# RWKV recurrence with two feed-forward stages on one core: decay of the state moved to ScalarE, a smaller gate, no constant products, scans two chunks ahead

## The chip, the cores and the metric

The kernel runs on one core of one Trainium2 chip. The metric is the device time of one execution in microseconds. Engines are named as in the profile: PE is TensorE (PEld its weight loads), DVE VectorE, ACT ScalarE, POOL GpSimd, SP the queue that issues most transfers.

## The reference

Three stages follow one another, over 4 x 768 tokens of width 384 (8 heads of 48).

```python
# 1. recurrence, for every batch b and head h, with a 48 x 48 state
for t in range(S):
    cur = np.einsum('bhd,bhe->bhde', u[None] * kt, vt)
    y[:, :, t] = np.einsum('bhd,bhde->bhe', rt, state + cur)
    state = wt[:, :, :, None] * state + np.einsum('bhd,bhe->bhde', kt, vt)
# 2. one of 8 experts per token, for tokens whose skip score is above 0
logits = xc @ w_gate; e_idx = argmax(logits); gate_w = softmax(logits)[e_idx]
out = xc + gate_w * (relu(xc @ w1[e]) @ w2[e])
# 3. dense: h = x @ w_in; g = h * clip(h + 3, 0, 6) / 6; return g @ w_out
```

## The kernel before

The change lies in the first stage. It cuts the 768 steps into 6 chunks of 128 and takes them in the order chunk, batch: 24 pieces, numbered i, four to a round (one chunk of all four batches). Inside a piece the recurrence is products: with running products p of the decay w, the score matrix of a piece is (k scaled) by (r scaled), masked, times v, plus r times the state left by the piece four earlier.

One pass of the main loop works on several pieces at once, and the order of the code is the order on each engine (manual schedule). Per pass the engines do this:

- DVE: `state` adds the new outer products (in PSUM tile `sl`) to the old state (L569), and multiplies by the decay of the whole chunk (L573); `scan` forms the forward running product (L431), four pieces ahead of the state; `scan_end` bounds its last value from below (L436), `scan_inv` takes the inverse (L439), `scan_back` runs four scans backward (L446, four instructions); `masked` (L494, twice) evacuates the scores; `x_out` (L546) adds the diagonal part. Each fourth pass the gate's first half `gate_a`, each fourth its second, `gate_o` and `gate_b`, come in between.
- PE: `scores` (L490), four products of constants into the bank of the result (L524), `apply` in two halves (L529 with the state, L534 with v), `xpose` (L583) between the halves, `k_xpose` (L504, L507), `state_mm` (L558, L560), `logits` (L597), and each fourth pass `gate_rank`.
- ACT: `diag_v` (eight scaled copies, L478), copies of the state into the two diagonal blocks `sbd` (L574, L575), the decay `pc` (L467), evacuations (L585, L511, L514), and `w_hi` (L270), the upper half of an expert's weight.
- POOL: `scale` (L456, the products of r and k with p), `ru` (L470), a `scatter` of 128 finished tokens to their expert's rows (L663), and `w_lo` (L276), the lower half of a weight, in 12 passes from the tenth on.
- SP: loads of a piece's r, k and w (`ch`, 3 buffers), of v, of raw weights, stores of the result, and in passes 2 to 5 zero rows for the scatter's target.

After the last piece the gate of the last chunk is done in two halves (batches 0 and 1, then 2 and 3), the last tokens are scattered, and the second stage loads them (`xw`), transposes them (L815 to L817) and multiplies. There the weights' lower halves are formed on DVE.

Of the kernel before, what the change touches and what calls it, by code (L numbers as in the profile page):

```python
# [19 lines left out]
E, F = 8, 1024  # L20
# [16 lines left out]

P_LO = 1e-16
# [4 lines left out]
DG = 2  # L43
W0 = 7
# [165 lines left out]
def rwkv_moe_kernel(ctx: ExitStack, tc: tile.TileContext, ch, vt, u, w9, wx, wm, out):  # L210
# [19 lines left out]
    cum = const.tile([128, E1], BF16, name="cum")  # L230
# [114 lines left out]
    with tc.manual_schedule():  # L345
# [8 lines left out]
        nc.vector.memset(cum, 0.0)  # L354


        with ExitStack() as p1:
            wpool["raw"] = p1.enter_context(tc.tile_pool(name="rawp", bufs=3))
# [42 lines left out]
            one, zero, pgp = cb[0:PP, 0:1], cb[0:PP, 1:2], cb[0:PP, 8:12]  # L401
            dkp = cb[:, 16:48].rearrange("p (b e) -> p b e", b=B)
            cmp_, s4p, cumf, stp = cb[:, 48:52], cb[:, 52:56], cb[:, 64:73], cb[0:PP, 128:320]
            stp = stp.rearrange("p (a d) -> p a d", a=PR)
            sl = ps_s.tile([128, 512], F32, tag="sl", name="sl")
            st = [fx.tile([PP, PR, D], F32, name=f"st{b}") for b in range(B)]
            cdt = [fx.tile([128, B, E1], F32, name=f"cd{j}") for j in range(2)]
            sbd = [fx.tile([PP, PR, 2 * D], F32, name=f"sbd{b}") for b in range(B)]
# [3 lines left out]
            nc.vector.memset(cumf, 0.0)  # L412
# [6 lines left out]
            for t in cdt:  # L419
                nc.vector.memset(t, 0.5)  # L420
            nc.gpsimd.iota(ids, pattern=[[C, NCH], [S, B]], base=0, channel_multiplier=1)
            nc.gpsimd.iota(zrow[:, 385:386].bitcast(I32), pattern=[[0, 1]], base=BIGI, channel_multiplier=1)

            pw, pcw, rtw, ktw, ruw, dgw, dvw, atw, ktT, xt4, lgp, xTs, scw, xw, rkw_ = ({} for _ in range(15))
# [36 lines left out]
            def scale_rest(i):  # L461
                rc = chb.pop(i)
                rkw_.pop(i)
                pe = pw.pop(i)[1]
                if i // B < NCH - 1:
                    pc = wk.tile([PP, PR], F32, tag="pc", name="pc", bufs=4)
                    nc.scalar.activation(out=pc, in_=pe, func=ACTF.Copy)  # L467
                    pcw[i] = pc
                ru = wk.tile([PP, PR, C], F32, tag="ru", name="ru", bufs=3)
# [92 lines left out]

            def state(i):
                c, b = divmod(i, B)
                if c < NCH - 1:
                    sp = sl[0:PP, 0:PR * D].rearrange("p (a d) -> p a d", a=PR)
                    pcb = pcw.pop(i).to_broadcast([PP, PR, D])
# [6 lines left out]
                    nc.scalar.activation(out=sbd[b][0:48, :, 0:D], in_=st[b][0:48], func=ACTF.Copy)  # L574
                    nc.scalar.activation(out=sbd[b][64:112, :, D:2 * D], in_=st[b][64:112], func=ACTF.Copy)  # L575
                elif ok(i + 4):
                    scan(i + 4)
# [10 lines left out]
            def logits(i):  # L588
                c, b = divmod(i, B)
                xT = xTs.pop(i)  # L590
                b0 = 2 if i >= NST - 2 else 0
# [9 lines left out]


            def gate_a(c, b0, nb):
# [10 lines left out]
                ex = sm.tile([128, B, E], F32, tag="ex", name="ex")[:, 0:nb, :]  # L614
                nc.scalar.activation(out=ex, in_=dl, func=ACTF.Exp)
                cd = cdt[(c + b0 // 2) % 2][:, 0:nb, :]
# [4 lines left out]
                od = sm.tile([128, B, E1], BF16, tag="od", name="od")[:, 0:nb, :]  # L621
# [4 lines left out]
            def gate_rank(c, b0, nb):  # L626
# [4 lines left out]
                nc.tensor.matmul(rnk, ones, cum[:, None, :].to_broadcast([128, nb, E1]), start=True, stop=False)  # L631
# [5 lines left out]


            def gate_o(c, b0, nb):
                ex, od = gw.pop((c, b0))  # L640
                o1 = sm.tile([128, B, E1], F32, tag="o1", name="o1")[:, 0:nb, :]
                nc.vector.tensor_tensor(out=o1, in0=rkw.pop((c, b0)), in1=od, op=ALU.mult)
                gw[c, b0] = ex, od, o1

            def gate_b(c, b0, nb):
                xt = xt4[c][:, b0:b0 + nb, :]
                ex, od, o1 = gw.pop((c, b0))
                s4 = s4p[:, 0:nb]
                nc.vector.tensor_reduce(out=s4, in_=ex, axis=AX.X, op=ALU.add)
                nc.vector.tensor_scalar(out=s4, in0=s4, scalar1=1e-9, scalar2=None, op0=ALU.add)  # L650
                nc.vector.reciprocal(out=xt[:, :, DM], in_=s4)
                si = sm.tile([128, B], I32, tag="si", name="si")[:, 0:nb]
                with nc.allow_low_precision(reason="one term of the sum is not zero, a whole number"):
                    nc.vector.tensor_reduce(out=si, in_=o1, axis=AX.X, op=ALU.add)
                siw[c, b0] = si
                sd = sm.tile([128, E1], F32, tag="sd", name="sd")
                nc.vector.tensor_reduce(out=sd, in_=od.rearrange("p b e -> p e b"), axis=AX.X, op=ALU.add)
                nc.vector.tensor_tensor(out=cumf, in0=cumf, in1=sd, op=ALU.add)
                nc.vector.tensor_copy(out=cum, in_=cumf)

            def scatter(c, b):
                b0 = 2 if c == NCH - 1 and b >= 2 else 0
# [4 lines left out]

            wq = [(0, q) for q in ORD] + [(1, q) for q in range(4)]
            rq = list(wq)
# [4 lines left out]
            for i in range(-3, NST + 1):  # L674
                if i >= W0 + 2 and wq:
                    w_hi(*wq[0])
# [6 lines left out]
                if ok(i + 3):  # L683
                    scan_end(i + 3)
                    scan_inv(i + 3)
                    if i + 3 > 0:
                        scan_back(i + 3)
                if i == -3:
# [3 lines left out]
                    scale_rest(0)  # L692
                if i == 1 - 3:
                    scale(1)
                    scale_rest(1)
# [5 lines left out]
                if i == -1:  # L701
                    scores(1)
                    for g in range(2):
                        masked(1, g)
                if ok(i + 2) and i >= 0:
                    scale(i + 2)
                    scale_rest(i + 2)
                if 7 <= i < NST - 1:
                    scatter(*divmod(i - 7, B))
                if i == NST - 1:  # L710
                    for b in range(B):
                        scatter(NCH - 2, b)
                if i < 2 - 3:
                    load_ch(i + 3 + 3)
                if ok(i + 5) and i >= 0:
                    load_ch(i + 5)
                if i >= 6 and (i - 6) % 4 == 0 and i < NST:
                    gate_o((i - 6) // 4, 0, B)
                if i > 0 and ok(i + 1):
# [6 lines left out]
                if i >= W0 + 2 and wq:  # L726
                    w_lo(*wq.pop(0), nc.gpsimd)
                if i >= W0 and rq:
                    w_raw(*rq.pop(0))
                if i >= 5 and (i - 5) % 4 == 0 and i < NST:  # L730
                    gate_a((i - 5) // 4, 0, B)
                if i >= 6 and (i - 6) % 4 == 0 and i < NST:
                    gate_b((i - 6) // 4, 0, B)
                if i > 0 and ok(i + 1):
# [6 lines left out]
                if ok(i):  # L741
# [3 lines left out]
                if i == NST - 1:  # L745
                    logits(i - 2)
                    gate_a(NCH - 1, 0, 2)
                    logits(i - 1)
                elif ok(i - 1) and i < NST - 2:
                    logits(i - 1)  # L750
                if i >= 5 and (i - 5) % 4 == 0 and i < NST:
# [5 lines left out]
                for k in range(1, i + 6) if i == -3 else (i + 5,):  # L757
                    if ok(k):
                        load_v(k)
            gate_rank(NCH - 1, 0, 2)  # L760
            gate_o(NCH - 1, 0, 2)
            gate_b(NCH - 1, 0, 2)
            logits(NST - 1)
            for b in range(2):
                scatter(NCH - 1, b)
            warm1(4, "sc0")
            for f in (gate_a, gate_rank, gate_o, gate_b):
                f(NCH - 1, 2, 2)
            for b in range(2, B):
                scatter(NCH - 1, b)  # L770
            warm1(4, "sc0")

# [208 lines left out]
        def flag_sum():  # L981
            p = ps.tile([128, 512], F32, tag="tp1", name="fs")[0:1, 0:E1 + 2]
            nc.tensor.matmul(p[:, 0:E1], ones[:, 0:1], cum, start=True, stop=True)
# [93 lines left out]
```

## Time and profile before

| | |
|---|---|
| median of 3 runs | 760.44 us (758.36 to 762.3) |
| profiled execution, its own time | 762.69 us |
| span of the profiled execution | 761.0 us |
| granted TensorE clock over the span | 0.988 |
| PE, DVE, ACT, POOL busy | 734.3, 497.3, 346.9, 219.0 us |

The profiled execution is 2.25 us above the median; 1.69 us of its time lie outside the span. The recurrence takes the first 159 us or so, the experts and the dense stage the rest. Shares of busy time mix these stages, so the rows further down are taken from the stretches that the change touches.

### The profile page before, as it was taken

To read this page: it belongs to the slowest core of one execution; us is meant where nothing else is said; L and a number is where in the kernel's file an instruction comes from. 1 tells how busy PE (TensorE), PEld (TensorE's weight loads), DVE (VectorE), ACT (ScalarE), POOL (GpSimd) and SP (SyncE) were. 2 spreads that over 40 slices of the span, in tenths; PEclk is the share of its full clock that TensorE was granted. 3 is DMA by queue.
4 is the path that set the end of the run, shared out by engine and by line. 5 is a ranking of instruction groups with operands and counts; after the bars stand their busy time and mean duration, and the time that the engine had idled before them with its cause. 6 is when DMAs were issued, how large, how long until landed. Compare 5 with 4: busy or idle time off the path is not lost.

```text
span 761.0 us, 14589 instructions
## 1 busy us (share of the span) xinstructions
PE 734.3 (96%) x5653; PEld 604.8 (79%) x5653; DVE 497.3 (65%) x974; ACT 346.9 (46%) x796; POOL 219.0 (29%) x192
## 2 busy tenths in 40 slices
PE   7999999989999997989999999999999999999995
PEld 3788888859999997957777888888888888788884
DVE  8989999837999999927885454455445434333331
ACT  2666777626566666326554333333233333333331
POOL 3758999942344444303441000000000000000000
PEclk9999999999999999989999999999999999999998
DMA  8699888328787873042230220221022010001001
GB/s 233 206 300 264 246 243 251 112 86 287 249 276 238 288 250 143 13 159 62 85 103 13 77 68 13 79 66 37 2 90 67 25 54 1 1 0 43 0 1 46
DMA packets 40590, 90.84 MB, mean 119 GB/s; under 512 B 5442, under 2 KB 19552, under 8 KB 40512
## 3 DMA queue, kind: packets, MB, share of 16 engines
q1 hardware_dynamic: 37952, 85.14, 36.6%
q0 software_dynamic: 2560, 4.69, 1.7%
q8 instruction: 46, 0.75, 0.4%
q14 instruction: 32, 0.26, 0.1%
HBM read 72.51 MB, written 20.53 MB: 122 GB/s over the span
## 4 chain that ended last, share of the span: by engine, by line
PE 69%; DVE 21%; DMA 3%; ACT 2%; issue 2%; SPq 1%; POOL 0%; DVEq 0%; ACTq 0%
PE f L787 8%; PE f L788 8%; PE f L790 8%; PE acc L950 8%; PE acc L952 8%; PE acc L949 8%; DVE wlo L276 5%; PE sc L490 4%; PE x L534 3%; PE x L529 3%; PE x L524 2%; DVE wlo L327 2%; DVE hl L828 2%; DVE a L304 2%; DVE a L307 2%
## 5 line engine op out<-in xcount | busy, mean ns | idle before, releaser
L935 DVE SCALAR_TENSOR_TENSOR f<-t,f 128x512 f32<-128x512 f32 x96 | 66.6, 694 | 130.5 <-ACT t L934 130.5
L934 ACT ACTIVATE t<-f,three 128x512 f32<-128x512 f32 x96 | 66.0, 688 | 160.1 <-PE f L790 160.1
L950 PE MATMUL acc<-gh,wlo 128*128 128x512 f32 x288 | 115.0, 399 | 2.0 <-DVE wlo L327 1.8
L787 PE MATMUL f<-bh,whi 128*128 128x512 f32 x288 | 115.6, 401 | 0.6 <-ACT bh L922 0.6
L949 PE MATMUL acc<-gh,whi 128*128 128x512 f32 x288 | 115.7, 402 | 0.0
L788 PE MATMUL f<-bh,wlo 128*128 128x512 f32 x288 | 115.1, 400 | 0.0
L937 DVE TENSOR_TENSOR gl<-f,gh 128x512 fp32r<-128x512 f32 x96 | 66.4, 691 | 63.8 <-ACT gh L936 63.8
L936 ACT ACTIVATE gh<-f 128x512 fp32r<-128x512 f32 x96 | 57.4, 598 | 100.3 <-DVE f L935 100.3
L952 PE MATMUL acc<-gl,whi 128*128 128x512 f32 x288 | 84.0, 396 | 0.0
L790 PE MATMUL f<-bl,whi 128*128 128x512 f32 x288 | 83.6, 399 | 0.0
L950 PEld LDWEIGHTS acc<-gh,wlo 128*128 128x128 f32 x288 | 54.3, 188 | 17.5 <-DVE wlo L327 5.5
L314 POOL TENSOR_TENSOR lf<-lf,ab 128x384 f32<-128x384 f32 x32 | 32.5, 1015 | 121.0 <-DVE ab L308 100.1
L787 PEld LDWEIGHTS f<-bh,whi 128*128 128x128 f32 x288 | 54.9, 190 | 14.3 <-ACT bh L922 1.0
L276 DVE TENSOR_TENSOR wlo<-raw,whi 128x768 fp32r<-128x768 f32 x52 | 66.0, 1270 | 0.0
L788 PEld LDWEIGHTS f<-bh,wlo 128*128 128x128 f32 x288 | 55.0, 191 | 13.3
L790 PEld LDWEIGHTS f<-bl,whi 128*128 128x128 f32 x288 | 54.6, 190 | 13.4
L952 PEld LDWEIGHTS acc<-gl,whi 128*128 128x128 f32 x288 | 54.2, 188 | 13.2
L270 ACT ACTIVATE whi<-raw 128x768 fp32r<-128x768 f32 x64 | 54.1, 845 | 23.4 <-DMA raw<-in_wx_dram 23.1
L949 PEld LDWEIGHTS acc<-gh,whi 128*128 128x128 f32 x288 | 54.3, 189 | 11.8
L787 PE MATMUL f<-xh,whi 128*128 128x256 f32 x192 | 50.1, 290 | 6.1 <-DVE hl L828 5.3
L456 POOL TENSOR_TENSOR rkt<-ch,p 112x1024 f32<-112x1024 f32 x22 | 48.0, 2181 | 25.1 <-DVE p L446 14.3
L788 PE MATMUL f<-xh,wlo 128*128 128x256 f32 x192 | 48.7, 282 | 0.0
(149 smaller groups left out, 1410.9 us busy)
## 6 DMA issues: line engine op xcount, KB each, us to landing
raw<-in_wx_dram SPq DMA_DIRECT2D x64, 384.0 KB, 4.8
ch<-in_ch_dram SPq DMA_DIRECT2D x23, 674.2 KB, 5.9
draw<-in_wm_dram SPq DMA_DIRECT2D x32, 384.0 KB, 4.4
cw<-in_ch_dram SPq DMA_DIRECT2D x24, 226.2 KB, 2.6
v<-in_vt_dram SPq DMA_DIRECT2D x24, 192.0 KB, 3.9
xo<-xt SPq DMA_DIRECT2D x24, 192.0 KB, 3.2
xb<-xo SPq DMA_DIRECT2D x24, 192.0 KB, 3.8
out_dram<-y SPq DMA_DIRECT2D x17, 256.0 KB, 2.2
```

Of the source, the lines that this page charges most:

```text
L270: nc.scalar.activation(out=hi, in_=t, func=ACTF.Copy)
L276: (eng or nc.vector).tensor_tensor(out=lo, in0=t, in1=hi.bitcast(F32), op=ALU.subtract)
L787: nc.tensor.matmul(o, wh, xh, start=(i == 0), stop=False)
L788: nc.tensor.matmul(o, wl, xh, start=False, stop=False)
L790: nc.tensor.matmul(o, wh, xl, start=False, stop=(i == len(ws) - 1))
L934: nc.scalar.activation(out=t, in_=p, func=ACTF.Relu, bias=three)
L935: nc.vector.scalar_tensor_tensor(out=p, in0=t, scalar=6.0, in1=p, op0=ALU.min, op1=ALU.mult)
L936: nc.scalar.activation(out=hi, in_=p, func=ACTF.Copy)
L937: nc.vector.tensor_tensor(out=lo, in0=p, in1=hi.bitcast(F32), op=ALU.subtract)
L949: nc.tensor.matmul(acc[k][m], wh[:, os_[m]:os_[m] + 128], hi, start=(j == 0), stop=False)
L950: nc.tensor.matmul(acc[k][m], wl[:, os_[m]:os_[m] + 128], hi, start=False, stop=False)
L952: nc.tensor.matmul(acc[k][m], wh[:, os_[m]:os_[m] + 128], lo, start=False, stop=(j == 15))
```

## The change

The multiplication of the state by the chunk's decay leaves DVE for ACT, as four scaled copies (one for each pair of heads). DVE keeps the sum, now written to SBUF (a copy in the first round). The bound before the inverse (`scan_end`) is gone. The gate loses three small instructions per round: the 1e-9 of the sum stands as a ninth column of `ex`, and the running count of tokens is reduced together with the one-hot rows. The four constant products ahead of `apply` are gone. A piece's scan is made two pieces ahead, not three or four, and its loop starts at -2. `w_lo` stands on POOL in every second pass, eight times in all; the remaining four weights are split after the last gate, by ACT and DVE. The last gate is cut into three batches and one.

```diff
@@ scan @@
-            def scan_end(i):
-                nc.vector.tensor_scalar(out=pgp, in0=pw[i][1], scalar1=P_LO, scalar2=None, op0=ALU.max)
             def scan_inv(i):
                 nc.vector.reciprocal(out=pw[i][0][:, 516:1032].rearrange("p (a b) -> p a b", a=PR)[:, :, 127],
-                                     in_=pgp)
+                                     in_=pw[i][1])
@@ apply @@
-                    for _ in range(4):
-                        nc.tensor.matmul(xw[i].rearrange("p (a b) -> p a b", a=3), ones,
-                                         ones[:, None, :].to_broadcast([128, 3, 128]), start=True, stop=True)
@@ state @@
+            def state_sum(i):
+                b = i % B
+                sp = sl[0:PP, 0:PR * D].rearrange("p (a d) -> p a d", a=PR)
+                s = wk.tile([PP, PR, D], F32, tag="stp", name="stp")
+                if i < B:
+                    nc.vector.tensor_copy(out=s, in_=sp)
+                else:
+                    nc.vector.tensor_tensor(out=s, in0=sp, in1=st[b], op=ALU.add)
+                stw[i] = s
+
             def state(i):
-                    if c:
-                        nc.vector.tensor_tensor(out=stp, in0=sp, in1=st[b], op=ALU.add)
-                        sp = stp
-                    if ok(i + 4):
-                        scan(i + 4)
-                    nc.vector.tensor_tensor(out=st[b], in0=sp, in1=pcb, op=ALU.mult)
+                b = i % B
+                s, pc = stw.pop(i), pcw.pop(i)
+                for pr in range(PR):
+                    nc.scalar.activation(out=st[b][:, pr, :], in_=s[:, pr, :], func=ACTF.Copy, scale=pc[:, pr:pr + 1])
...
@@ gate @@
+            def gate_s(c, b0, nb):
+                s4 = s4p[:, 0:nb]
+                nc.vector.tensor_reduce(out=s4, in_=gw[c, b0][0], axis=AX.X, op=ALU.add)
+                nc.vector.reciprocal(out=xt4[c][:, b0:b0 + nb, DM], in_=s4)
...
-                nc.vector.tensor_scalar(out=s4, in0=s4, scalar1=1e-9, scalar2=None, op0=ALU.add)
...
-                nc.vector.tensor_reduce(out=sd, in_=od.rearrange("p b e -> p e b"), axis=AX.X, op=ALU.add)
-                nc.vector.tensor_tensor(out=cumf, in0=cumf, in1=sd, op=ALU.add)
-                nc.vector.tensor_copy(out=cum, in_=cumf)
+                    nc.vector.tensor_reduce(out=odt[(j + 1) % 2][:, 0, :],
+                                            in_=odt[j % 2][:, 0:nb + 1, :].rearrange("p b e -> p e b"),
+                                            axis=AX.X, op=ALU.add)
@@ main loop @@
             wq = [(0, q) for q in ORD] + [(1, q) for q in range(4)]
-            rq = list(wq)
+            wat = {6 + 2 * k: p for k, p in enumerate(wq[0:8])}
-            for i in range(-3, NST + 1):
-                if ok(i - 1):
-                    state(i - 1)
-                elif ok(i + 3):
-                    scan(i + 3)
+            for i in range(-2, NST):
+                if i in wat:
+                    w_hi(*wat[i])
                 if ok(i):
                     diag_v(i)
+                if ok(i + 2):
+                    scan(i + 2)
+                if ok(i - 1) and i - 1 < NST - B:
+                    state_sum(i - 1)
+                if ok(i + 2):
+                    scan_inv(i + 2)
+                    if i > -2:
+                        scan_back(i + 2)
...
+                if i >= 0 and ok(i + 1):
+                    r_k(i + 1)
...
+                if i in wat:
+                    w_lo(*wat[i], nc.gpsimd)
...
+                if i >= 0 and ok(i + 2):
+                    scale(i + 2)
+                    scale_end(i + 2)
...
+                if ok(i - 1) and i - 1 < NST - B:
+                    state(i - 1)
...
+            for p in wq[8:12]:
+                w_hi(*p)
+                w_lo(*p)
```

DVE in a pass without gate work, in the third round, before:

```order
L569 TENSOR_TENSOR cb<-sl,st_151 112x192
L431 SCALAR_TENSOR_TENSOR p<-ch,cb 112x516
L573 TENSOR_TENSOR st_151<-cb,pc 112x192
L436 TENSOR_SCALAR cb<-p 112x4
L439 RECIPROCAL p<-cb 112x4
L446 SCALAR_TENSOR_TENSOR p<-ch,p,cb 112x127 x4
L494 TENSOR_TENSOR at<-sc_1080,mask 128x4x128
L494 TENSOR_TENSOR at<-sc_1081,mask 128x4x128
L546 TENSOR_TENSOR xt<-x,dv 128x384
```

And DVE in the same pass of the changed kernel (its lines are numbered anew; `stp` is the sum's new tile):

```order
L428 SCALAR_TENSOR_TENSOR p<-ch,cb 112x516
L563 TENSOR_TENSOR stp<-sl,st_149 112x192
L434 RECIPROCAL p<-p 112x4
L441 SCALAR_TENSOR_TENSOR p<-ch,p,cb 112x127 x4
L491 TENSOR_TENSOR at<-sc_1068,mask 128x4x128
L491 TENSOR_TENSOR at<-sc_1069,mask 128x4x128
L539 TENSOR_TENSOR xt<-x,dv 128x384
```

Two instructions are gone, and the forward scan now stands ahead of the sum that reads PE's result in `sl`.

ACT in a pass with a weight's upper half (`whi`), before:

```order
L270 ACTIVATE whi<-raw 128x768
L478 ACTIVATE dv<-v,dg 128x48 x8
L574 ACTIVATE sbd_155<-st_149 48x4x48
L575 ACTIVATE sbd_155<-st_149 48x4x48
L467 ACTIVATE pc<-p 112x4
L585 ACTIVATE xT<-xp 128x384
L511 ACTIVATE kT<-kp 128x448
L514 ACTIVATE dg<-kp 128x8
```

And ACT in such a pass of the changed kernel:

```order
L265 ACTIVATE whi<-raw 128x768
L475 ACTIVATE dv<-v,dg 128x48 x8
L461 ACTIVATE pc<-p 112x4
L570 ACTIVATE st_150<-stp,pc 112x48 x4
L571 ACTIVATE sbd_160<-st_150 48x4x48
L572 ACTIVATE sbd_160<-st_150 48x4x48
L580 ACTIVATE xT<-xp 128x384
L508 ACTIVATE kT<-kp 128x448
L511 ACTIVATE dg<-kp 128x8
```

Four products of the state have come in ahead of the copies to `sbd` and of the evacuation `xT` that PE's `logits` wait for; passes with `whi` now alternate with passes without.

POOL in two passes of the third round, before:

```order
L456 TENSOR_TENSOR rkt<-ch,p 112x1024
L470 TENSOR_TENSOR ru<-ch 112x512
L663 DMA xs<-xt,si 24576x388
L276 TENSOR_TENSOR wlo<-raw,whi 128x768
L456 TENSOR_TENSOR rkt<-ch,p 112x1024
L470 TENSOR_TENSOR ru<-ch 112x512
L663 DMA xs<-xt,si 24576x388
L276 TENSOR_TENSOR wlo<-raw,whi 128x768
```

And in two passes of the changed kernel:

```order
L467 TENSOR_TENSOR ru<-ch 112x512
L659 DMA xs<-xt,si 24576x388
L451 TENSOR_TENSOR rkt<-ch,p 112x1024
L467 TENSOR_TENSOR ru<-ch 112x512
L659 DMA xs<-xt,si 24576x388
L271 TENSOR_TENSOR wlo<-raw,whi 128x768
L451 TENSOR_TENSOR rkt<-ch,p 112x1024
```

`rkt`, which needs the scan of the same pass, now stands last in the pass, and `wlo` is there in every second one.

## Rows read from the trace of the kernel before

**Rows 1.** The page's first line.

```profile
span 761.0 us, 14589 instructions
```

**Rows 2.** Busy time of each engine in stretches of the recurrence, TensorE's clock, DMA.

```profile
core 0: us, PE busy (x) PEld busy (x) DVE busy (x) ACT busy (x) POOL busy (x), PEclk, DMA share, GB/s
77.32:102.64 25.32, 25.32 (x483) 21.01 (x482) 23.52 (x64) 18.20 (x62) 24.41 (x19) 1.00 0.90 251
52.00:77.32 25.32, 25.32 (x483) 21.04 (x482) 23.52 (x64) 16.54 (x59) 18.58 (x15) 1.00 0.91 255
...
44.07:145.79 101.72, 101.72 (x1954) 84.69 (x1953) 94.00 (x249) 70.63 (x239) 88.30 (x64) 1.00 0.85 242
```

**Rows 3.** The chain that ended last, two passes: start us, us, what.

```profile
65.07 1.09 PE sc L490 x16
66.16 0.76 PE x L524 x4
...
71.18 1.09 PE sc L490 x16
...
83.88 1.50 PE sc L490 x16
```

**Rows 4.** DVE's timeline, one pass: start us, us, what, idle before.

```profile
60.81 0.33 DVE L573 TENSOR_TENSOR st<-cb,pc 112x192 f32<-112x192 f32 x1
61.18 0.17 DVE L436 TENSOR_SCALAR cb<-p 112x4 f32<-112x4 f32 x1
...
65.12 0.37 DVE L569 TENSOR_TENSOR cb<-sl,st 112x192 f32<-112x192 f32 x1 [0.29 <-PE sl L597]
```

**Rows 5.** DVE's timeline, first gate instruction of gate_b and what follows it.

```profile
82.35 0.18 DVE L649 TENSOR_REDUCE cb<-ex 128x4 f32<-128x32 f32 x1
...
83.49 0.68 DVE L494 TENSOR_TENSOR at<-sc,mask 128x512 f32<-128x512 f32 x1
```

**Rows 6.** POOL's timeline, one pass with a weight's lower half.

```profile
101.61 2.18 POOL L456 TENSOR_TENSOR rkt<-ch,p 112x1024 f32<-112x1024 f32 x1
...
106.25 1.82 POOL L276 TENSOR_TENSOR wlo<-raw,whi 128x768 fp32r<-128x768 f32 x1
...
108.02 2.18 POOL L456 TENSOR_TENSOR rkt<-ch,p 112x1024 f32<-112x1024 f32 x1
```

**Rows 7.** ACT's timeline in the same round.

```profile
96.23 0.84 ACT L270 ACTIVATE whi<-raw 128x768 fp32r<-128x768 f32 x1
...
96.97 1.90 ACT L478 ACTIVATE dv<-v,dg 128x48 f32<-128x48 f32 x8
...
99.13 0.36 ACT L575 ACTIVATE sbd<-st 48x192 f32<-48x192 f32 x1
```

**Rows 8.** DVE's timeline at the start: scan of piece 3, first result.

```profile
19.17 1.22 DVE L431 TENSOR_TENSOR_SCAN p<-ch,cb 112x516 f32<-112x516 f32 x1
...
22.35 0.53 DVE L546 TENSOR_TENSOR xt<-x,dv 128x384 f32<-128x384 f32 x1
```

**Rows 9.** Timelines after the last piece (DVE, POOL), and a group of the page.

```profile
159.25 0.56 DVE L546 TENSOR_TENSOR xt<-x,dv 128x384 f32<-128x384 f32 x1 [2.98 <-PE x L534]
...
173.20 1.02 DVE L817 TENSOR_TENSOR xl<-tp,xh 128x384 fp32r<-128x384 f32 x2 [8.32 <-ACT xh L816]
...
166.44 0.97 POOL L663 DMA_INDIRECT xs<-xt,si  x1 [0.30 <-issue]
...
L276 DVE TENSOR_TENSOR wlo<-raw,whi 128x768 fp32r<-128x768 f32 x52 | 66.0, 1270 | 0.0
```

**Rows 10.** Start of the kernel: PE's timeline, and one stretch of Rows 2's view.

```profile
14.36 2.15 PE L490 MATMUL sc<-rkt 48*128 48x128 f32 x16 [2.05 <-DVE at L494]
...
13.54:16.95 3.41, 2.48 (x18) 1.79 (x19) 3.31 (x8) 0.40 (x2) 0.00 (x0) 0.80 1.01 276
```

**Rows 11.** Passes with zero rows: one stretch, and the issues' sizes and landing times.

```profile
40.00:50.00 10.00, 10.00 (x191) 8.15 (x187) 7.63 (x20) 6.80 (x25) 3.75 (x5) 1.00 1.05 334
...
xs<-zrow SPq DMA_DIRECT2D x8, 388.0 KB, 6.1
```

More of the change, by code (lines that the diff above doesn't have):

```diff
@@ L36 @@
 BIGW = 1e20
-P_LO = 1e-16
 TB = 16
@@ L407, in rwkv_moe_kernel @@
             cdt = [fx.tile([128, B, E1], F32, name=f"cd{j}") for j in range(2)]
+            ext = [fx.tile([128, B, E1], F32, name=f"ex{j}") for j in range(2)]
+            odt = [const.tile([128, B + 1, E1], BF16, name=f"od{j}") for j in range(2)]
             sbd = [fx.tile([PP, PR, 2 * D], F32, name=f"sbd{b}") for b in range(B)]
@@ L636, in gate_rank @@
                                      start=False, stop=(b == nb - 2))
+            def gate_s(c, b0, nb):
+                s4 = s4p[:, 0:nb]
+                nc.vector.tensor_reduce(out=s4, in_=gw[c, b0][0], axis=AX.X, op=ALU.add)
+                nc.vector.reciprocal(out=xt4[c][:, b0:b0 + nb, DM], in_=s4)
             def gate_o(c, b0, nb):
                 ex, od = gw.pop((c, b0))
+                j = gate_n(c, b0)
                 o1 = sm.tile([128, B, E1], F32, tag="o1", name="o1")[:, 0:nb, :]
                 nc.vector.tensor_tensor(out=o1, in0=rkw.pop((c, b0)), in1=od, op=ALU.mult)
[L643 to L649, printed above, removed]
-                nc.vector.tensor_scalar(out=s4, in0=s4, scalar1=1e-9, scalar2=None, op0=ALU.add)
-                nc.vector.reciprocal(out=xt[:, :, DM], in_=s4)
                 si = sm.tile([128, B], I32, tag="si", name="si")[:, 0:nb]
-                with nc.allow_low_precision(reason="one term of the sum is not zero, a whole number"):
+                with nc.allow_low_precision(reason="sums of whole numbers below 256, or of one term"):
                     nc.vector.tensor_reduce(out=si, in_=o1, axis=AX.X, op=ALU.add)
+                    nc.vector.tensor_reduce(out=odt[(j + 1) % 2][:, 0, :],
+                                            in_=odt[j % 2][:, 0:nb + 1, :].rearrange("p b e -> p e b"),
+                                            axis=AX.X, op=ALU.add)
                 siw[c, b0] = si
-                sd = sm.tile([128, E1], F32, tag="sd", name="sd")
-                nc.vector.tensor_reduce(out=sd, in_=od.rearrange("p b e -> p e b"), axis=AX.X, op=ALU.add)
-                nc.vector.tensor_tensor(out=cumf, in0=cumf, in1=sd, op=ALU.add)
-                nc.vector.tensor_copy(out=cum, in_=cumf)
             def scatter(c, b):
-                b0 = 2 if c == NCH - 1 and b >= 2 else 0
+                b0 = 3 if c == NCH - 1 and b == 3 else 0
                 ins = nc.gpsimd.indirect_dma_start(
@@ L700, in rwkv_moe_kernel @@
                     warm1(WN)
[L701 to L707, printed above, removed]
+                if i >= 0 and ok(i + 1):
+                    r_k(i + 1)
                 if 7 <= i < NST - 1:
                     scatter(*divmod(i - 7, B))
-                if i == NST - 1:
+                if last:
                     for b in range(B):
                         scatter(NCH - 2, b)
[L713 to L717, printed above, removed]
+                if i in wat:
+                    w_lo(*wat[i], nc.gpsimd)
+                if i + 2 in wat:
+                    w_raw(*wat[i + 2])
+                if i >= NST - 4:
+                    w_raw(*wq[i - NST + 12])
+                if i >= 0 and ok(i + 2):
+                    scale(i + 2)
+                    scale_end(i + 2)
+                if i == -2:
+                    load_ch(3)
+                if i >= 0 and ok(i + 4):
+                    load_ch(i + 4)
+                if ok(i - 1) and i - 1 < NST - B:
+                    state(i - 1)
+                if i >= 6 and (i - 6) % 4 == 0:
                     gate_o((i - 6) // 4, 0, B)
-                if i > 0 and ok(i + 1):
+                if i >= 0 and ok(i + 1):
                     scores(i + 1)
@@ L725, in rwkv_moe_kernel @@
                     xpose(i - 1)
[L726 to L730, printed above, removed]
+                if i >= 5 and (i - 5) % 4 == 0:
                     gate_a((i - 5) // 4, 0, B)
[L732 to L734 removed]
+                if i >= 0 and ok(i + 1):
                     masked(i + 1, 1)
@@ L740, in rwkv_moe_kernel @@
                     k_xpose(i + 1)
-                if ok(i):
+                if ok(i) and i < NST - B:
                     state_mm(i)
@@ L744, in rwkv_moe_kernel @@
                     warm1(WN)
-                if i == NST - 1:
-                    logits(i - 2)
-                    gate_a(NCH - 1, 0, 2)
+                if ok(i - 1):
                     logits(i - 1)
-                elif ok(i - 1) and i < NST - 2:
-                    logits(i - 1)
-                if i >= 5 and (i - 5) % 4 == 0 and i < NST:
+                if i >= 5 and (i - 5) % 4 == 0:
+                    gate_s((i - 5) // 4, 0, B)
                     gate_rank((i - 5) // 4, 0, B)
```

88 lines of the change are left out of this document (40 added, 48 removed).

## The prediction

> **What bounds the kernel now.** I looked at the recurrence alone, since all edits lie there, and began with the busy time of each engine per round of four passes. A round takes 25.32 us, and two rounds in a row take just that although POOL is busy 18.58 us in the one and 24.41 in the other [rows 2]. So POOL is not what sets the pace, nor ACT with 18.20. PE shows 25.32 of 25.32 and DVE 23.52. PE's ends are modelled, so a full PE alone proves nothing; I therefore read the chain of waits next. It stays on PE from one pass to the next: scores at 65.07, constant products at 66.16 for 0.76, scores again at 71.18, which makes 6.11 us a pass [rows 3]. DVE in the same stretch stands waiting for PE's `sl`, 0.29 us at 65.12 [rows 4]. Once a round it is the other way: the scores take 1.50 instead of 1.09 [rows 3], 0.41 us in which PE waits for their bank, which DVE empties. A round is then 4 x 6.11 + 0.41 = 24.85, and the remaining 0.47 are the gate's rank products. The reader should see a PE-bound loop with DVE and POOL close behind: what PE gains is only kept down to the next engine.
>
> **The changed round, engine by engine.**
>
> PE: four times 0.76 go [rows 3]. 25.32 - 3.04 = 22.28 with the 0.41 still in it, 21.87 without.
>
> DVE: the state's product goes, 0.37 from its start to the next instruction's, and the guard, 0.17 [rows 4]: 4 x 0.54 = 2.16. Of the gate's seven instructions, 1.14 us in all [rows 5], three have no successor: 0.49. Busy time falls from 23.52 to 20.87. The round had 1.80 us of DVE idle [rows 2]; if half of it is the bare gap between instructions, the floor is 21.8 (20.9 to 22.7). The sum now stands behind the forward scan and no longer waits at `sl`, behind which the scan and everything after it had been queued. The first round's sum becomes a copy of the same size and I price it alike.
>
> POOL: a pass with `wlo` takes 6.41 us from `rkt` to `rkt`, and `wlo` 1.77 of it [rows 6]. With two of four instead of four of four: 4 x 6.41 - 2 x 1.77 = 22.1.
>
> ACT: four scaled copies of 48 columns come in each pass. Eight like them take 1.90 us, so four take 0.95 [rows 7]; a round gets 3.80 more and loses two `whi` at 0.74 [rows 7]. 18.20 - 1.48 + 3.80 = 20.5 busy [rows 2]. Splitting costs: one copy of 192 columns takes 0.36 [rows 7], the four pieces 0.59 more than that. The Trainium skill (Perfetto Trace Analysis, Optimizing Scalar/DVE Operations) says that each ACT instruction on SBUF pays a fixed part of some 93 ns and that larger operations help where the engine is saturated. By that figure the split would cost 3 x 0.093 = 0.28 us a pass, an estimate from the page; the row's 0.59 is larger and the row decides. ACT's round would by the page be 4 x 0.31 = 1.2 us shorter, below POOL's either way, so the sum is the same by both. ACT is not saturated, but it runs in order: behind the products stand `sbd`, `xT` (for PE's logits) and `kT`. In a `whi` pass the entry is 0.74 + 0.95 later than without them, which could hold PE's logits by some 0.3 us. That is an estimate, and inside the bounds below.
>
> So four engines need 20.5 to 22.1 us. If nothing collides, a round takes POOL's 22.1. If POOL has no room to run late, a `wlo` pass costs its 6.41 and the others PE's 5.35: 2 x 6.41 + 2 x 5.35 + 0.47 = 24.0. There is some room: `rkt` for piece i+2 is needed only by the scores of the next pass. It has become less, because the scan that it waits for is now made in the same pass. I take the middle, 23.0.
>
> **The sum**, against the profiled execution's own 762.69 us (span 761.0, the rest outside it [rows 1]).
>
> Passes 5 to 20: the stretch from 44.07 to 145.79 is 101.72 us [rows 2], four rounds of 25.43. Four of 23.0 are 92.0: -9.7 (-13.3 to -5.7).
>
> Start: one whole scan leaves the way to the first result. From 19.17 to 22.35 it is 3.18 [rows 8], and three guards of 0.17 [rows 4] go too: first result at 18.7, -3.7. The scan is only put off, and has to fit into later passes; DVE's 21.8 beside 22.1 says it does. If it doesn't, 0.
>
> Passes 1 to 4: 22.35 to 44.07 [rows 2, 8]. PE would allow 4 x 0.76 less, but eight fills of 388 KB fall there, with the DMA engines already at a share of 1.05 and 334 GB/s [rows 11]. I take 0 (up to -1.5).
>
> Passes 21 to 23: 145.79 to 159.25 [rows 2, 9]. No scans are left, DVE waits 2.98 us for PE [rows 9], so three times 0.76 should be kept: -2.3 (0 to -2.3).
>
> The seam: the last scatter starts 7.2 us behind the last result [rows 9]. Three of its batches now go with the first gate and one with the second, which may bring the last scatter forward a little: -0.5 (0 to -1.0). The four late splittings cost DVE 4 x 1.27 = 5.1 us, and lie in the 8.32 us that it waits there for ACT [rows 9]. Without that cover they would cost up to 5.1. The raw weights for them are loaded two passes ahead or more; the load of a piece is issued one piece later than before, and has two passes to land.
>
> The stages behind are not touched and start earlier. Sum: -9.7 - 3.7 - 2.3 - 0.5 = -16.2, so 746.5 by its own time. That execution lies 2.25 us above the median of 760.44, so I predict 744.2. The ends add to -5.7 and -21.8, or 754.7 and 738.6.
>
> **Rivals.**
>
> A. Another engine takes the loop over: POOL in `wlo` passes, or ACT in `whi` passes holding PE's logits. For it speaks that four engines come within 1.6 us of one another; against it that the old loop lost only 0.41 us a round beside its longest engine. A round is then 24.0, the start is paid back, the tail kept: 4 x 1.43 + 2.3 + 0.5 = 8.5 us faster, 752.
>
> B. TensorE's clock falls, and the kernel gets slower. At the start the trace shows it: PE stood idle for 2.05 us until 14.36, in the stretch from 13.54 the granted clock averages 0.80 (a part of it at 1.2 GHz, half of 2.4), and sixteen score products take 2.15 us there [rows 10] against 1.09 later [rows 3]. The constant products are work that keeps PE active, and they go. A pass of 5.35 us of PE work would cost up to 5.35 more at 1.2 GHz; three passes of 24 at half clock eat the whole gain, and ten would give 760.4 - 16.2 + 53.5 = 797.7. Against it: the removed 0.76 us also shorten the pass, so PE has 5.35 of 5.75 us to do, and idle stretches as long as the one at 14.36 do not appear in the loop. The Trainium skill (TensorE: Matmul & The Clock Gate, What's actually happening) puts it as a default that is throttled and released by activity; by that rule, too, it is a question of how much PE work is left.
>
> C. The constant products were free. If PE had really been waiting for DVE within those 0.76 us, only DVE's 2.65 us a round count: 4 x 2.65 = 10.6 and the start's 3.7 is not kept, since DVE then has to make the scan up: 10.6 + 0.5 = 11 faster, 749. If neither DVE nor PE set the pace, the change does nothing: within 4 us of 760.4. The chain on PE speaks against that.
>
> **Numbers.** My forecast, a gain of 10 to 20 us: 0.56. A: 0.22. C with DVE's part alone: 0.10. More than 20: 0.03. Nothing (the end of C): 0.04. B: 0.05. What a measurement of this kernel tells from no change is about 0.5%, 3.8 us. Faster by more 0.91, within it 0.04, slower 0.05. The range 738.5 to 754 takes in the bounds of the sum, A and C's first case, and leaves B, the null case and the far end out.
>
> **What the changed profile would show.** Right: first result near 18.7, rounds of about 23 us, last result near 143; clock 1.0 through the recurrence; PE still on the chain but with POOL or DVE pieces in it; DVE's late `wlo` ahead of the first transposed tokens. Wrong: waits of PE's logits for ACT's `xT`, rounds of 24 or more (A); a clock under 1.0 between 20 and 140 us (B); `ch` loads that land late in passes 2 to 8 and hold the scan; transposes at the seam that wait for the four late splittings.

## The result

The changed kernel takes 755.47 us (median of five runs, 747.32 to 770.85) beside 762.3 of the kernel before on the same chip, a ratio of 0.9863 with a 95% interval of 0.9827 to 0.99; the ratio, here and below, leaves out the runs in which TensorE's clock was down most. At the 760.44 us of the forecast that ratio makes 750.0: faster, inside the range, short of the forecast by 6 us. The five runs go with their mean clock: 747.32 us at 0.99, 770.85 at 0.95, so 0.01 of clock is worth 5.9 us. The profiled run took 768.31 us.

The page's span and row of the clock, in 40 slices; beside them stands [rows 1]:

```profile
span 766.6 us, 14383 instructions
...
PEclk8996599889999999989999999999999999999998
```

Stretches by pass (from result to result, L539) in the columns of [rows 2]; the last row is a whole round:

```profile
52.65:58.09 5.44, 5.18 (x115) 4.55 (x111) 4.80 (x12) 4.75 (x18) 1.99 (x2) 1.00 1.08 313
58.09:67.71 9.62, 6.81 (x96) 5.98 (x94) 4.88 (x11) 5.70 (x19) 9.22 (x6) 0.71 1.03 281
67.71:77.28 9.57, 9.57 (x116) 8.53 (x117) 5.84 (x16) 4.97 (x19) 6.59 (x8) 0.50 0.63 177
77.28:87.34 10.06, 10.06 (x122) 8.92 (x122) 5.67 (x16) 5.35 (x19) 6.73 (x5) 0.50 0.47 157
87.34:96.72 9.38, 9.38 (x117) 8.38 (x117) 4.94 (x11) 4.74 (x18) 3.72 (x4) 0.53 0.42 129
...
102.05:123.92 21.87, 21.87 (x468) 19.54 (x468) 20.85 (x52) 20.43 (x76) 20.60 (x17) 1.00 0.84 250
```

The profile holds two kinds of passes. An undisturbed round takes 21.87 us where it took 25.32 [rows 2]. The four passes from 58.09 to 96.72 take 38.63 us, 16.8 more than such a round, most of it at 1.2 GHz. PE is shown busy in every microsecond of the last three of them: a busy PE says nothing of its speed, the PEclk column does (0.50 is 1.2 GHz).

What stands ahead of the fall, and of a second one near the end, from the timelines of POOL, DVE and PE (columns as in [rows 4]):

```profile
58.26 1.18 POOL L659 DMA_INDIRECT xs<-xt,si  x1 [3.62 <-DMA raw<-in_wx_dram]
59.47 2.18 POOL L451 TENSOR_TENSOR rkt<-ch,p 112x1024 f32<-112x1024 f32 x1
...
62.26 1.23 DVE L428 TENSOR_TENSOR_SCAN p<-ch,cb 112x516 f32<-112x516 f32 x1 [3.62 <-DMA ch<-in_ch_dram]
...
61.70 1.74 PE L487 MATMUL sc<-rkt 48*128 48x128 f32 x16 [2.81 <-POOL rkt L451]
...
144.24 1.83 POOL L271 TENSOR_TENSOR wlo<-raw,whi 128x768 fp32r<-128x768 f32 x1
146.03 2.17 POOL L451 TENSOR_TENSOR rkt<-ch,p 112x1024 f32<-112x1024 f32 x1
...
148.25 2.07 PE L487 MATMUL sc<-rkt 48*128 48x128 f32 x15 [1.40 <-POOL rkt L451]
...
167.88 1.74 POOL L659 DMA_INDIRECT xs<-xt,si  x1 [0.30 <-issue]
169.93 1.43 POOL L659 DMA_INDIRECT xs<-xt,si  x1 [0.31 <-DVE wlo L271]
...
166.96 3.55 DVE L271 TENSOR_TENSOR wlo<-raw,whi 128x768 fp32r<-128x768 f32 x4
```

The first scatter waits 3.62 us for transfers (it may write only when the zero rows are down); `rkt` stands behind it on POOL, PE's scores wait 2.81 us for `rkt`, and sixteen of them then take 1.74 us and more against 1.09 [rows 3]. In the same passes `ch` comes late and holds the scan. In pass 20 `wlo` stands ahead of `rkt`, and PE waits 1.40 us. At the seam to the second stage the last two scatters take 1.74 and 1.43 us beside DVE's late `wlo`, where one took 0.97 [rows 9].

The prediction's sum, piece by piece (us; e1 is another profile of the same kernel, e12 the last experiment):

| stretch | before | predicted | after | e1 | e12 |
|---|---|---|---|---|---|
| first result at | 22.35 | 18.7 | 19.29 | 18.36 | 18.48 |
| passes 1 to 4 | 21.72 | 21.7 | 20.36 | 19.06 | 20.08 |
| passes 5 to 20 | 101.72 | 92.0 | 105.98 | 92.81 | 88.89 |
| passes 21 to 23 | 13.46 | 11.2 | 16.63 | 21.12 | 13.57 |
| last result to last scatter | 7.19 | 6.7 | 7.67 | 7.47 | 8.91 |
| last scatter at | 166.44 | 150.3 | 169.93 | 158.82 | 149.93 |

### The profile page after: what moved, and what is told of

Same layout as the page of the kernel before. It is cut to its first block, busy times and chain, and to the rows that moved or that the text cites. A ratio compares the mean times of both kernels' runs of the same rounds, so it can differ in the third digit from the quotient of the medians.

```text
span 766.6 us, 14383 instructions
## 1 busy us (share of the span) xinstructions
PE 736.0 (96%) x5557; PEld 614.0 (80%) x5557; DVE 489.0 (64%) x918; ACT 364.6 (48%) x876; POOL 212.6 (28%) x188
## 4 chain that ended last, share of the span: by engine, by line
PE 47%; DVE 21%; DMA 3%; ACT 3%; issue 2%; SPq 0%; DVEq 0%; ACTq 0%
PE f L786 8%; PE f L787 8%; PE f L789 8%; PE acc L949 8%; PE acc L951 8%; PE acc L948 8%; DVE wlo L271 6%; DVE hl L827 2%; DVE wlo L322 2%; DVE a L299 2%; DVE a L302 2%; DMA draw<-in_wm_dram 1%; DVE f L934 1%; DVE gl L936 1%; ACT gh L935 1%
## 5 line engine op out<-in xcount | busy, mean ns | idle before, releaser
L271 DVE TENSOR_TENSOR wlo<-raw,whi 128x768 fp32r<-128x768 f32 x56 | 69.7, 1249 | 0.0
```

What stands on the lines that cost most here:

```text
L271: (eng or nc.vector).tensor_tensor(out=lo, in0=t, in1=hi.bitcast(F32), op=ALU.subtract)
```

## The experiments

Two theories of where the expected gain went. **K**: the constant products kept TensorE's clock up; without them it falls. **F**: the falls begin with stalls that the new order makes (zero rows and `ch` loads in passes 5 to 8, `rkt` behind other work on POOL, the last passes). The kernels e1 to e4, e5 to e8, e9 to e11 and e12 ran side by side with the kernel before, which took 766.05, 768.22, 767.24 and 760.98 us there, so ratios are compared, not times. A splitting below is `w_hi` and `w_lo` of one weight; pass i ends with the result of piece i.

**e1: the changed kernel again.** No edit.

> The changed kernel once more, beside the next three on one chip. Its five runs on record lie between 747.3 and 770.9 us with a mean clock of 0.99 to 0.95, and its profile shows 34 us at half clock from 62 us on. Theory K (the clock: without the constant products a stall of some 3 us lets TensorE's clock fall, and the loop's own products don't bring it back soon) and theory F (the stalls: zero rows fill the DMA engines in passes 2 to 5, piece loads land late, and the first scatter waits for the zero rows ahead of rkt on POOL) both expect the same spread again: 747 to 771, each microsecond at half clock costing about 0.4 us.

758.71 us, ratio 0.9887 (0.9855 to 0.992). The falls move from run to run: here the clock is down in some passes near 60 us and in the last ones.

```profile
43.45:130.23 86.78, 83.89 (x1751) 74.74 (x1747) 77.71 (x190) 75.97 (x277) 77.99 (x58) 0.96 0.90 262
130.23:139.24 9.01, 7.14 (x99) 6.31 (x95) 5.65 (x17) 3.21 (x13) 8.64 (x9) 0.62 0.25 79
139.24:147.75 8.51, 6.89 (x118) 6.00 (x115) 2.66 (x8) 2.58 (x10) 4.66 (x5) 0.80 0.40 130
```

**e2: the constant products put back.**

```diff
                     xw[i] = ps_x.tile([128, DM], F32, tag="x", name="x")
+                    for _ in range(4):
+                        nc.tensor.matmul(xw[i].rearrange("p (a b) -> p a b", a=3), ones,
+                                         ones[:, None, :].to_broadcast([128, 3, 128]), start=True, stop=True)
```

> The changed kernel with the four constant products ahead of apply put back, and nothing else. Theory K: the stall in pass 7 is still there, but the clock is back at 2.4 GHz within 7 us; mean clock 0.98 to 0.99 in all runs, their spread below 0.5%; an undisturbed round is 21.87 + 4 x 0.76 = 24.9 us, so the time is 760 less 3 at the start and 4 x 0.5 in the rounds, about 755. Theory F: the clock falls as often as without the products, runs vary by 3% as before, and each round costs 3 us more on top: 757 to 780.

765.99 us, ratio 0.9992 (0.997 to 1.0013), runs within 6.6 us of one another, clock 0.978 to 0.988. A round of its profile:

```profile
94.62:119.50 24.88, 24.88 (x484) 20.77 (x484) 21.19 (x52) 20.53 (x75) 21.53 (x17) 1.00 0.73 225
```

All the other edits together make 0.44 us a round when PE keeps its constant products. PE alone sets this loop; DVE's 21.19 us of work are no bound. The steady clock is what K expected, the 755 us that it named did not come.

**e3: the scatter behind `rkt` on POOL.** The two lines with `scatter(*divmod(i - 7, B))` moved from ahead of `scale(i + 2)` to behind it.

> The changed kernel with the scatter moved behind rkt on POOL, so that a scatter that waits for zero rows no longer holds the product that PE's scores wait for. Theory F: PE's wait of 2.8 us for rkt in pass 8 and the clock's fall after it are gone, all runs near 745 to 748 with clock 0.985 or more. Theory K: late piece loads remain and still make PE stand for over a microsecond here and there, the clock falls in some runs, times between 745 and 770.

760.07 us, ratio 0.9876 (0.9845 to 0.9907): no change. The wait for zero rows no longer holds `rkt`, but the late load does the same by way of DVE: the scan waits 2.65 us, PE's transposes wait 1.78 us for an instruction that stands behind the scan on DVE, and the clock is at half in the pass behind.

```profile
47.68 1.23 DVE L428 TENSOR_TENSOR_SCAN p<-ch,cb 112x516 f32<-112x516 f32 x1 [2.65 <-DMA ch<-in_ch_dram]
...
51.01 0.60 PE L501 MATMUL kp<-ident,rkt 112*128 112x112 f32 x4 [1.78 <-DVE o L648]
...
52.43:60.19 7.76, 7.76 (x96) 7.00 (x95) 4.88 (x11) 4.96 (x18) 4.59 (x4) 0.50 1.08 272
```

**e4: the kernel before without its constant products.** The same loop as in e2, taken out of the kernel before.

> The kernel before without its four constant products, and nothing else (the products' result is overwritten, so nothing is left out of the computation). Its scans stay three and four ahead and POOL has rkt ahead of the scatter. Theory K: long stretches at half clock appear here too, runs vary by over 1%, and the median is no better than 760. Theory F: without the stalls the clock holds, mean 0.985 or more; a round falls from 25.3 to what DVE and POOL leave, 24 to 25, and the time to 752 to 757.

768.5 us, ratio 1.0035 (1.0008 to 1.0062), clock 0.942 to 0.968 against 0.979 to 0.992 of the kernel before. Two rounds in a row, then PE's wait ahead of 25 us at half clock, and these:

```profile
49.75:75.01 25.26, 22.68 (x467) 20.14 (x466) 23.43 (x64) 15.99 (x58) 18.86 (x15) 1.00 1.04 295
75.01:99.37 24.36, 23.70 (x467) 21.09 (x466) 23.34 (x63) 17.80 (x62) 23.28 (x19) 0.93 0.83 250
...
98.22 0.26 PE L554 MATMUL sl<-v,kT 128*64 128x48 f32 x1 [0.66 <-DVE dl L608]
...
99.37:124.42 25.05, 25.05 (x304) 22.23 (x304) 17.46 (x46) 12.63 (x43) 20.89 (x15) 0.52 0.74 216
```

The first round stays at 25.26 us: PE has 2.6 us less to do and stands still that much longer, 1.4 us of it for DVE and 1.18 us without a semaphore. The second takes 24.36 us although the clock is down for some 3 us of it; DVE is busy for 23.34 of them. So e2 and e4 are the two halves of the change: the one alone gives 0.44 us a round, the other 0.06 and 0.96, both together 3.45. The long stretches at half clock and the spread (764.82 to 780.75 us) are what K expected, and they come in the old order: the new one is not needed for a fall.

**e5: zero rows earlier and thinner.**

```diff
-                for e in range(2 * i - 4, 2 * i - 2) if 2 <= i < 6 else ():
+                for e in {0: (0, 1), 1: (2, 3), 2: (4,), 3: (5,), 4: (6,), 5: (7,)}.get(i, ()):
```

> The changed kernel with the eight zero-row fills issued earlier and thinner: two after passes 0 and 1, one after passes 2 to 5, in place of two after passes 2 to 5. Theory F (the falls of TensorE's clock begin with stalls that the fills make): the first scatter on POOL no longer waits 2.7 us or more for the zero rows, the scores' wait of 1.9 us before 58 us goes, the clock stays at 1.0 between 45 and 100 us, and the time falls by some 4 us against the changed kernel's 758.7, with fewer long runs (ratio to before about 0.983). Theory K (without the constant products the clock falls whatever the transfers do): the clock falls again between 50 and 70 us although the scatter does not wait, and the ratio stays at 0.988.

755.99 us, ratio 0.985 (0.9804 to 0.9896), 0.004 under e1's, intervals overlapping. What F expected of this stretch is there: the first scatter waits 0.41 us, PE waits for no `rkt` here, and the clock is 1.00.

```profile
52.26 1.17 POOL L659 DMA_INDIRECT xs<-xt,si  x1 [0.41 <-DVE p L428]
...
44.06:68.94 24.88, 23.19 (x481) 20.49 (x481) 21.06 (x52) 20.23 (x75) 20.49 (x16) 1.00 0.93 271
```

The last passes still take 7.76 and 8.82 us.

**e6: pass 20 without a splitting.**

```diff
-            wat = {6 + 2 * k: p for k, p in enumerate(wq[0:8])}
+            wat = {6 + 2 * k: p for k, p in enumerate(wq[0:7])}
-                if i >= NST - 4:
+                if i >= NST - 5:
-            for p in wq[8:12]:
+            for p in wq[7:12]:
```

> The changed kernel with the splitting of pass 20 moved behind the recurrence: seven pieces in the loop, five at the end. Both theories say that the scores' wait of 1.4 us for POOL's rkt in pass 20 goes. Theory F: with it goes the half clock from about 132 to 146 us, passes 21 to 23 take 5.4, 4.8 and 3.6 us in place of 9.0, 8.5 and 3.6, last result some 8 us earlier; one more late wlo costs DVE 1.27 us at the seam, so about 5 us are left (ratio 0.981). Theory K: with PE's work smaller in the last passes, the clock falls there anyway, and the ratio stays at 0.988 to 0.99.

755.79 us, ratio 0.9858 (0.9813 to 0.9902). The scores' wait is gone and pass 21 takes 5.62 us in place of 9.01, but pass 22 now takes 9.20: PE stops there without waiting for a semaphore, and the clock falls behind that.

**e7: the state's product back on DVE.**

```diff
+            def state_dve(i):
+                nc.vector.tensor_tensor(out=st[i % B], in0=stw.pop(i), in1=pcw.pop(i).to_broadcast([PP, PR, D]),
+                                        op=ALU.mult)
+
             def state(i):
                 b = i % B
-                s, pc = stw.pop(i), pcw.pop(i)
-                for pr in range(PR):
-                    nc.scalar.activation(out=st[b][:, pr, :], in_=s[:, pr, :], func=ACTF.Copy, scale=pc[:, pr:pr + 1])
...
                     state_sum(i - 1)
+                    state_dve(i - 1)
```

> The changed kernel with one part undone: the state's product again on DVE (one instruction of 192 columns), none on ScalarE. If PE alone sets the round, rounds stay at 21.9 to 22.3 us and the time is the changed kernel's (ratio 0.988). If DVE is next as the prediction's floors have it, DVE's 20.85 busy becomes 22.3 and the floor with its gaps 23.3: rounds of 22.5 to 23.3, 2 to 5 us slower than the changed kernel (ratio 0.991 to 0.995). If the waits that this makes bring TensorE's clock down as well, slower than that.

790.55 us, ratio 1.0159 (1.0104 to 1.0215), slower than both kernels. The first passes, at full clock, take 5.42 us where e1's take 4.74: DVE sets them (busy for 15.88 of the 16.25 us from 26.26 to 42.51). Most of the rest is clock: down from 71 to 126 us, and again from 153 on; the fastest run, 776.17 us, has a mean clock of 0.961.

```profile
77.82:116.55 38.73, 38.73 (x467) 34.48 (x467) 25.33 (x55) 16.69 (x59) 22.01 (x18) 0.50 0.46 144
```

**e8: constant products in passes 4 to 8 and 19 to 23 alone.** e2's edit with `range(4 if 4 <= i <= 8 or i >= 19 else 0)`.

> The changed kernel with the four constant products back in passes 4 to 8 and 19 to 23 alone, where the waits of PE stand. Theory K (PE's missing work is what lets the clock fall): the clock stays at 1.0 between 45 and 145 us, the rounds between take 21.9; ten times 0.76 us come back, and what the half clock had cost (8 to 20 us) goes: ratio about 0.982, spread of the runs 7 us at most in place of 20. Theory F (the waits alone do it, whatever PE has to do besides): the waits of 1.9 and 1.4 us remain and the clock falls behind them as in the changed kernel; the ratio is 0.99 or above.

760.62 us, ratio 0.9912 (0.9874 to 0.9951). Runs lie closer (757.3 to 768.34), but both falls are there, behind a wait for `rkt` of 1.02 us at 60.04 and behind stops of PE at 144 to 148 us. In the passes between the clock holds, though only the last two of this stretch have constant products:

```profile
58.03:65.97 7.94, 6.92 (x107) 5.37 (x106) 4.90 (x11) 5.69 (x19) 7.74 (x5) 0.79 1.02 258
82.47:133.20 50.73, 50.19 (x1061) 44.06 (x1062) 46.70 (x113) 46.10 (x167) 48.98 (x37) 1.00 0.83 245
```

F's 0.99 came, and K in its simple form falls: constant products in the pass of a stall don't keep the clock up, and passes without them and without stalls keep it.

**e9: e5 and e6 together.**

> The changed kernel with both edits of the runs before: zero-row fills earlier, and the splitting of pass 20 behind the recurrence. Theory F: the two effects add, no scores wait for rkt between 40 and 145 us, TensorE's clock holds until pass 22; of the half clock only what follows PE's own stalls without a semaphore (about 143 to 151 in the run before) is left. About 6 us under the changed kernel, ratio 0.980 to 0.984. Theory K: the clock falls elsewhere instead, and the ratio stays at 0.985 to 0.989.

750.18 us (748.07 to 753.07), ratio 0.9769 (0.9732 to 0.9807), clearly under e1's. No fall until pass 22. What is left is PE's stop, from the timelines of PE and POOL:

```profile
138.29 0.29 PE L504 MATMUL kp<-u_sb,ru 112*64 112x2 f32 x4 [0.38 <-issue]
139.05 0.32 PE L504 MATMUL kp<-u_sb,ru 112*64 112x2 f32 x5 [0.46 <-issue]
...
141.27 0.29 PE L592 MATMUL sl<-w_sb,xT 128*64 128x9 f32 x4 [0.55 <-issue]
142.69 0.51 PE L592 MATMUL sl<-w_sb,xT 128*64 128x9 f32 x6 [1.13 <-issue]
...
135.50 1.01 POOL L659 DMA_INDIRECT xs<-xt,si  x1 [0.17 <-issue]
136.81 0.97 POOL L659 DMA_INDIRECT xs<-xt,si  x1 [0.30 <-issue]
...
140.65 0.98 POOL L659 DMA_INDIRECT xs<-xt,si  x1 [0.30 <-issue]
```

PE gets four or five instructions at a time, some 0.7 us apart, while POOL runs five scatters in a row.

**e10: the late splittings on POOL.** As e9, with `w_lo(*p, nc.gpsimd)` in the last loop.

> As the run before, with the five late splittings on POOL behind the last scatter in place of DVE. If DVE's late wlo slow the last scatters (1.43 to 1.74 us where 0.97 is usual, and a wait of 0.3), the last two take 0.97 here, and the last scatter starts 6.4 us behind the last result in place of 7.6: 1 us faster than the run before. Against it: POOL's five take 9 us, and the raw buffers come free later for the stage behind; then no change or 1 us slower. PE's stalls without a semaphore in pass 22 stay as they are, as does the half clock behind them.

753.2 us, ratio 0.9769 (0.9727 to 0.9812). The last scatters take 0.97 us each and the last one starts 6.89 us behind the last result, 7.47 in e9: so DVE's `wlo` had slowed them, and the time doesn't show it. PE's stops stay. In this profile the clock also fell near 60 us, behind a stop of PE of 1.26 us at 55.85.

**e11: splittings between the last scatters.** As e10, with:

```diff
+                if i == NST - 2:
+                    w_lo(*wq[7], nc.gpsimd)
                 if last:
                     for b in range(B):
                         scatter(NCH - 2, b)
+                        if b < 2:
+                            w_lo(*wq[8 + b], nc.gpsimd)
...
-            for p in wq[7:12]:
+            for p in wq[10:12]:
```

Their upper halves are made at the start of the same passes.

> As the run before, but three of the five late splittings now stand on POOL between the scatters of the last passes, so that these no longer run back to back. If PE's stalls without a semaphore (5 to 6 us of pieces of 0.7 us in passes 21 to 22) come of five scatters in a row, under which PE's instruction transfers come 11 us apart in place of 6 to 7, they go, passes 22 and 23 take 4.8 and 3.6 us in place of 9 and 4.6, and the clock holds to the end of the recurrence: 5 to 6 us faster than the run before, ratio 0.975. If the scatters have nothing to do with it, the stalls stay in the same pass, and the ratio is that of the run before, within 0.003.

745.79 us, ratio 0.9724 (0.9673 to 0.9775), below e10's 0.9769 with intervals that overlap. No stop of PE without a semaphore is left in the last passes; passes 22 and 23 take 3.89 and 3.83 us at full clock, 9.20 and 4.62 in e9:

```profile
134.59:138.48 3.89, 3.63 (x79) 3.28 (x79) 2.53 (x9) 2.28 (x9) 3.70 (x4) 1.00 0.51 159
138.48:142.31 3.83, 2.91 (x75) 2.56 (x71) 0.56 (x1) 3.47 (x12) 3.47 (x4) 1.00 0.60 182
```

**e12: two splittings between them in place of three.** As e10, with a splitting behind the scatters of batches 0 and 2.

> As the run before, with two splittings between the scatters of the last passes in place of three (two scatters in a row, a splitting, two, a splitting, one). If a row of scatters is what holds PE's instructions up, rows of two are short enough: no stalls of PE without a semaphore in passes 21 to 23, passes 22 and 23 below 5 us each, clock 1.0 to the last result, and the last scatter 1.8 us earlier behind the last result than the 9.3 us of the run before: ratio 0.970 to 0.973. If the three splittings helped by something else (their share of the late work), the stalls come back, and the ratio is 0.977 as with no gaps.

746.35 us (743.71 to 757.65), ratio 0.9814 (0.9782 to 0.9847): the ratio missed, beside a kernel before that is 6 us faster than in e11; by its ratio alone e12 is no better than e9. The stops are gone as expected, passes 22 and 23 take 4.12 and 3.83 us, and the last scatter starts 8.91 us behind the last result (9.33 in e11; the hoped-for 1.8 us is 0.4). The ratios of both lie below e1's.

## Why the prediction was right, and where it was not

**PE as the bound: right.** e2 settles it: with the constant products left in, everything else is worth 0.44 us a round. Rival C (constant products free, DVE's part alone 2.65 a round) is out. That DVE stands close behind is right too (e4: 25.26 and 24.36 us without them).

**The round: mis-sized.** 23.0 taken, 21.6 to 22.4 measured where the clock held; 21.87 is PE's own floor. The step that failed is the margin for POOL: priced with every `wlo` pass at 6.41 us, it showed 20.6 us busy and kept up. Four such passes are 25.64 us, more than the whole round and than the 24.41 of [rows 2]; those 24.41 less two `wlo` are 20.9. Rival A did not come: PE hardly waited for `xT` in the loop (0.45 us at most, once each in e1, e3 and e5).

**Start and passes 1 to 4.** -3.7 forecast, -3.1 and -4.0 measured. The 0 for passes 1 to 4 was too careful by 1.4 to 2.7: the transfers did not take back all that PE had gained there.

**Rival B, in part.** The step that failed is its "against": that idle stretches as long as the 2.05 us of [rows 10] do not appear in the loop. One of 2.81 us appeared, and the clock fell behind shorter ones too (1.40 us; 0.66 in e4). From 67.71 to 96.72 us PE is shown busy throughout, and the clock stays near half. The Trainium skill (TensorE: Matmul & The Clock Gate, What's actually happening) says that activity releases the throttle; these rows don't show it so. With the pass ahead this makes 34 us at half clock, worked out as (1 - PEclk) x 2 x length row by row, and the 16.8 us above, waits included. The reading that fits all runs, though none isolates it: not the constant products themselves had kept the clock up, but that PE was the longest. With 25.32 us of its own work a round its trace shows no wait from 44.07 to 145.79 us. Once its work is 21.87, whatever comes late on POOL, DVE or the transfers stops PE. The prediction named late `ch` loads as a sign and said that the scores' room behind `rkt` had shrunk, and gave neither a price in half clock.

**The last passes: wrong sign.** -2.3 forecast, +3.2 and +7.7 measured: the wait behind `wlo` in pass 20 (e6), and PE's stops (e11). Without both, e12's three passes take 13.57 us, nothing gained. The step that failed is "no scans are left". They were gone in the kernel before, whose last one starts in pass 20; made two pieces ahead instead of three, it starts in pass 21 of the changed kernel, where DVE is then busy for 5.45 of 5.62 us. That pass took 4.51 before; pass 22 gains 1.29. The kernel before, then e12 (DVE's timeline and a stretch in the columns of [rows 2] for each):

```profile
141.17 1.23 DVE L431 TENSOR_TENSOR_SCAN p<-ch,cb 112x516 f32<-112x516 f32 x1
...
145.79:150.30 4.51, 4.46 (x82) 3.59 (x81) 2.73 (x11) 2.07 (x9) 4.38 (x5) 1.00 0.15 49
...
127.92 1.22 DVE L428 TENSOR_TENSOR_SCAN p<-ch,cb 112x516 f32<-112x516 f32 x1
...
127.45:133.07 5.62, 4.95 (x118) 4.47 (x114) 5.45 (x16) 3.13 (x13) 5.42 (x6) 1.00 0.40 128
```

**The seam: wrong.** -0.5 forecast, +0.5 and +0.3 measured. The late splittings were said to lie in DVE's wait of 8.32 us; they do, but beside the last scatters, which they slow (e10). The Trainium skill (GPSIMD Engine Reference, Specifications) says that POOL's access to SBUF is shared with DVE and contends with DVE instructions of two SBUF inputs; the rows agree: 1.43 and 1.74 us beside `wlo`, 0.97 without.

**The sum.** The time lies inside the range in part by luck: the rounds came out shorter than taken, and the half clock, which stood in the sum at nothing, and the last passes took more than that back. Over a third of the forecast 16.2 us is missing (10.4 are left by the ratio); the rows put it down to waits, the clock behind them, and the last passes. e12's last scatter starts at 149.93 us, the forecast's at 150.3; that is luck too, for its terms are off by -1.6, -3.1, +2.4 and +2.2 us (second to fifth row of the table), and e12 is a kernel with other fills and splittings.

Open: why the clock came back after 7 us in one run and after 34 in another, with PE shown busy in both; and why it fell behind one stop and not behind another, as 1.26 us at 55.85 in e10 and 1.26 at 56.53 in e5.

## What to carry to other kernels

When two engines are near the same length, taking work from either alone shows little (0.44, and 0.06 to 0.96 us a round here, 3.45 together): test such edits as a pair. Filler work on the longest engine can seem to cost just its time, yet it also hides every late piece of the others; before it goes, list what will stop the engine then, and price a stop with the half clock behind it. Look at the granted clock by pass, not over the span.

## What was not expected of the hardware

PE stopped without any semaphore: in the last passes single gaps up to 1.15 us, 0.7 us from one handful of instructions to the next. In e2, e3, e5, e6, e8, e9 and e10 it happened in or just behind five scatters in a row on POOL; in the last passes of e11 and e12, with splittings between them, it did not. Behind the last result those two have rows of six and five scatters without a stop, but PE has few instructions to take there. With four in a row it is in the profiles of e1 and e4 (in e7 one gap of 0.28 us), and not in those of the kernel before and of the changed kernel. Single stops come without such a row too (1.26 us at 56.53 in e5). The profile lists the transfers of instructions as queues of their own. For the same ten microseconds, 135 to 145, first e9:

```profile
q1 hardware_dynamic: 429, 0.79, 27.2%
q0 software_dynamic: 320, 0.50, 13.8%
```

and e11:

```profile
q1 hardware_dynamic: 720, 1.38, 43.8%
q0 software_dynamic: 192, 0.31, 8.3%
q8 instruction: 1, 0.02, 0.7%
q14 instruction: 1, 0.01, 0.3%
```

In e9 the profile lists no transfer of instructions in that time. That the scatters keep the fetch from being made fits, but it was only argued: the changed kernel has ten such microseconds too, 147 to 157, at half clock for most of them, and no stop of this kind. That splitting the row up removes the stops was shown, in one profile each of two kernels.
